# A fused attention and ReGLU kernel: batch 2 loaded last and transposed by the crossbar, a new order for the head, and an output lag that grows from 14 to 18

## The chip, the cores and the metric

The kernel runs on one core of one Trainium2 chip. The metric is the device time of one execution in microseconds (us). The kernel before the change took 221.94 us, the median of three runs that lay between 221.68 and 222.19.

The engines have short names in the profile. PE is TensorE, which does the matrix multiplications; PEld is its weight load, which runs beside the multiplications. DVE is VectorE, ACT is ScalarE, POOL is GpSimd, SP is SyncE. Transfers (DMA) are issued from the queues of SP, ACT and POOL.

## The reference

There are B = 8 batches and H = 8 heads, S = 512 rows of x and Ns = 32 rows of state for each, with head size D = 64.

```python
scale = 1.0 / np.sqrt(D)
a = softmax(scale * x @ state.T)            # over the 32 states
xread = a @ state                           # (B, H, 512, 64)
a2 = softmax(scale * state @ x.T)           # over the 512 rows
sread = a2 @ x                              # (B, H, 32, 64)
t = concat([xread, sread], axis=2)          # (B, H, 544, 64)
t = t.transpose(0, 2, 1, 3).reshape(B * 544, 512)
gate = np.maximum(t @ w_gate, 0.0)          # w_gate, w_val: 512 x 1536
val = t @ w_val
out = (gate * val) @ w_out                  # w_out: 1536 x 512
```

## The kernel before, in words

**The algebra.** The rows of xread are never formed. Since `xread = a @ state`, the product `xread @ w_gate` is `a @ (state @ w_gate)`. For each batch the kernel computes U, the 32 state rows of every head times w_gate and w_val, and then multiplies the softmax weights with U. The scores of both softmaxes are the same numbers, so one exponential serves both.

**The steps.** The head of the kernel is written as a list of words. A word is a step, its arguments, and after `@` the PSUM banks that it takes. The steps are: `dx` load x of a batch, `dw` load columns of w_gate (0) or w_val (1), `ds` load the rest of the state, `do` load rows of w_out; these loads are issued on the queue of POOL. `stc`, `stT` and `sto` convert and transpose the state and copy it into `stT`. `xT` transposes x of a batch on PE and `xo` copies it out of PSUM; `xd` (`x_trans_dma`) does the whole transposition instead by a DMA transpose on the queue of SP. `sc` computes scores, `ex` their exponentials, `nr` and `nx` sums, reciprocals and the product. `aT` with `ao` transposes the softmax weights on PE into `ans`, and `ad` does it by a DMA transpose on SP's queue. `c` with `co`, and `u` with `uo`, compute U for some columns and copy it out of PSUM (`c` takes gate and value columns together). `gv` is a slice, below, with `re` (relu) and `mu` (the product gate times value). `o` is an output piece and `of` the copy and the write of a finished output tile. `xp` copies x into a padded buffer `xa` on POOL, `sr` multiplies the exponentials with it on PE, and `sn` normalizes the result on VectorE. `spin` is a matmul on zeros whose result is used by nothing.

**The slices.** The 1536 hidden columns are cut into NF = 12 slices of 128. Slice number g = 12 b + jf is batch b, columns 128 jf and up: four matmuls of 128x512 (gate and value, two halves of the contraction), the relu on ScalarE, the product on VectorE into `h_sb`. Numbers 96 to 107 are the twelve slices of the sread rows of all batches.

**The pieces.** The 512 rows of a batch make four output tiles of 128 rows. Each tile is a sum over 12 slices in one PSUM bank, in three pieces of four matmuls: piece 12 b + 3 t + q is third q of tile t of batch b. The first piece of a tile (q = 0) asks for a bank, and after the last (q = 2) `fin_x` copies the tile out on ScalarE and writes it from SP.

**The loop.** The word list ends after 28 slices and 10 pieces. From slice `first` = 28 on a loop runs (lines 496 to 508): the slice; then one piece if `piece <= g - lag`, with `lag` 18; then the units planned for this slice; and, in slices in `paired`, a second piece behind the units. The units of batch s = 2 and up: score halves of the batch s + 1 (`att_half`); in slices jf = 7 and 10 a block of three `u` units of that batch (`u_block`), each with one copy on ScalarE and one on VectorE; the load, the DMA transpose and the pad copy of later batches; and `sr` of one batch: batch 2 in slice (2, 7), batch 3 in (2, 10), and each batch b from 4 on in (b - 1, 10). Slices jf = 7 and 10 of batches 2 to 6 are the paired ones. For slice (2, 7) the units stand in the order `u_block`, then `sr`, and then comes the second piece.

**The banks.** There are eight PSUM banks. In the loop, slices, U units and scores take banks 0 to 5 in turn, and output tiles banks 6 and 7 in turn. `sr` asks for a "spare" bank (lines 85 to 89):

```python
elif kind == "spare":
    n = 6 + turn["o"] % 2
else:
    n = turn["r"] % 6 if kind == "r" else 6 + turn["o"] % 2
    turn[kind] += 1
```

**What sets the order.** Each engine runs its instructions in the order in which the program gives them; nothing reorders them. Waits between engines are put in from the data: an instruction that writes a buffer or a bank waits for the earlier instructions that read it. Each queue of transfers issues in its own order too. POOL has eight semaphores for its loads, so a load waits until the eighth load before it has landed. The state transposes of batches 4 to 7 (`state_T_dma`) go through SP and their copies (`state_out_dma`) through POOL, both as units of slices of batch 2. After the loop come the output tiles of the sread rows (`fin_s`), the last pieces of batch 7, and the last tile in four column parts (`out_last`).

Of the kernel before, what the change touches and what calls it, by code (L numbers as in the profile page):

```python
# [16 lines left out]
def kernel(  # L17
# [203 lines left out]
    def x_pad(b):  # L221

        v = xa[:, b % NX].rearrange("p (c h) d -> p h c d", c=NC)[:, :, :, 0:D]
        nc.gpsimd.tensor_copy(out=v, in_=xb[b])  # L224
# [107 lines left out]
    def fin_x(b, tsub, eng="act"):  # L332
        o_sb = opool.tile([128, d_model], FP32, name="o_sb", tag="o_sb")
        copy[eng](out=o_sb, in_=held["o", b, tsub])  # L334
        n = 2 if 4 * B - 9 <= 4 * b + tsub < 4 * B - 4 else 1
# [74 lines left out]
    dx.1.0.2 dx.1.1.2 stc.0.0.act stc.0.1.act xc.0.0.dve dw.0.0.128 spin.7 stT.0@4 xc.0.1.act dw.1.0.128 on xT.0.0.4@2  # L410
    sto.0.0.dve sto.0.1.act xT.0.4.4@5 xo.0.0.4.dve dw.0.128.128 xo.0.4.4.dve dw.1.128.128 spin.1 sc.0.0@3 dw.0.256.256 ex.0.0 xT.0.8.4@0
    xT.0.12.4@1 xo.0.8.4.dve dw.1.256.256 xo.0.12.4.act nr.0.0 spin.2 sc.0.1@6 dw.0.512.256 xT.1.0.8@4 ex.0.1 nx.0.0
    xo.1.0.8.act nr.0.1 dw.1.512.256 spin.2 xT.1.8.8@2 xo.1.8.8.dve sc.1.0@5 dw.0.768.256 ex.1.0 nx.0.1 dw.1.768.256
    spin.2 c.0.0.128@30 sc.1.1@1 co.0.0.128.0.act nr.1.0 aT.0.1@6 co.0.0.128.1.act dw.0.1024.256 aT.0.0@4 ex.1.1
    ao.0.0.dve ao.0.1.act dw.1.1024.256 spin.1 c.0.128.128@25 c.1.0.128@30 nr.1.1 co.0.128.128.1.act gv.0.0@14
    co.0.128.128.0.act co.1.0.128.1.act nx.1.0 re.0.0 dw.0.1280.256 c.1.128.128@65 nx.1.1 gv.0.1@20 co.1.0.128.0.act
    co.1.128.128.0.act mu.0.0 co.1.128.128.1.act aT.1.1@7 re.0.1 dw.1.1280.256 aT.1.0@1 ao.1.1.act c.0.256.256@36
    ao.1.0.dve c.1.256.256@54 mu.0.1 co.0.256.256.0.act gv.1.1@21 dx.2.0.1 co.1.256.256.0.act co.0.256.256.1.dve
    re.1.1 gv.1.0@73 co.1.256.256.1.act mu.1.1 ds re.1.0 c.1.512.256@05 c.0.512.256@62 co.1.512.256.1.dve
    co.1.512.256.0.act gv.1.2@41 co.0.512.256.1.act mu.1.0 do.0.6 co.0.512.256.0.act gv.0.3@70 re.1.2 xp.1 gv.1.5@52  # L420
    re.0.3 mu.1.2 re.1.5 mu.0.3 gv.0.4@36 mu.1.5 re.0.4 xp.0 c.1.768.256@47 c.0.768.256@15 mu.0.4 co.1.768.256.0.act
    gv.0.2@03 co.0.768.256.0.act co.1.768.256.1.dve re.0.2 gv.0.5@26 do.6.12 co.0.768.256.1.act mu.0.2 gv.1.7@41 dx.3.0.1
    re.0.5 re.1.7 mu.0.5 gv.0.7@70 mu.1.7 re.0.7 gv.1.3@53 mu.0.7 re.1.3 gv.1.4@24 mu.1.3 re.1.4 gv.1.6@61 mu.1.4
    re.1.6 c.1.1280.256@70 c.0.1280.256@53 mu.1.6 co.1.1280.256.0.act c.1.1024.256@24 stc.1.0.pool xT.2.0.8@6
    co.0.1280.256.0.act co.1.1024.256.0.dve xT.2.8.8@1 co.0.1280.256.1.act co.1.1024.256.1.dve stc.1.1.pool
    c.0.1024.256@75 xo.2.8.8.act gv.0.10@23 co.1.1280.256.1.dve stc.3.1.pool co.0.1024.256.1.dve re.0.10 gv.1.9@40
    co.0.1024.256.0.act xo.2.0.8.dve stc.2.0.pool re.1.9 gv.0.6@12 mu.0.10 stc.3.0.pool re.0.6 mu.1.9 gv.0.11@57 mu.0.6
    stc.2.1.pool re.0.11 gv.0.8@64 mu.0.11 re.0.8 stT.1@3 gv.1.10@10 mu.0.8 sto.1.0.act sto.1.1.dve re.1.10 sc.2.0@2 o.0.0@7 ex.2.0
# [116 lines left out]
```

## Time and profile before

| what | value |
|---|---|
| median of three runs | 221.94 us (221.68 to 222.19) |
| the profiled execution, its own time | 222.66 us |
| the profiled execution, its span | 220.9 us |
| PE busy | 214.6 us, 97% of the span |
| DVE busy, ACT busy | 130.8 us, 123.5 us |
| a 128x512 matmul of `gv` or of an output piece | 380 ns each, the next starts 0.216 us after it |
| relu of a slice, product of a slice | 586 ns, 689 ns |
| landing of an x load of 512 KB, median | 7.1 us after its issue |
| landing of a weight load of 256 KB, median | 9.4 us (w_gate), 10.0 us (w_val) |
| landing of a DMA transpose of x | 4.4 to 8.0 us |
| landing of a DMA transpose of `ans` | 3.1 to 4.9 us |

A row of the profile in order of time begins with the start in us from the start of the span and the length in us; then follow the engine, the line of the kernel, the operation, the tile written and the tiles read, the shapes, and the number of instructions merged into the row. In brackets stand the idle time before the row and what ended it. Matmuls overlap, so a row of several matmuls ends later than the next row begins, and the pace of PE is read from start to start. The span is that of one execution; the device time of the same execution is 1.76 us longer.

### The profile page before, as it was taken

How to read it: one execution, taken by the hardware profiler on the slowest of the kernel's cores; microseconds unless marked ns; L12 is line 12 of the kernel's file. 1: busy time of each engine (PE TensorE's matmuls, PEld its weight loads, DVE VectorE, ACT ScalarE, POOL GpSimd, SP SyncE). 2: the span in 40 equal slices, each digit the busy share in tenths (PEclk: the TensorE clock that was granted, in tenths of full speed). 3: DMA queues.
4: the chain of work that ended last, by engine and by line, in shares of the span. 5: the costliest groups of instructions: out<-in, count | busy, mean ns of one | idle time of the engine just before them, and what ended most of it. 6: DMA issues, size and time to landing. Idle time of an engine off the chain costs nothing.

```text
span 220.9 us, 4858 instructions
## 1 busy us (share of the span) xinstructions
PE 214.6 (97%) x1955; PEld 105.2 (48%) x1955; DVE 130.8 (59%) x229; ACT 123.5 (56%) x236; POOL 40.6 (18%) x51
## 2 busy tenths in 40 slices
PE   7899999999999999999999999999999999999994
PEld 2553454444544444444444444445454445666543
DVE  5796898865787567664766487648665334222100
ACT  4699887465666565555566555646654543223221
POOL 7875830080035400040003000000000000000000
PEclk9999999999999999999999999999999999999999
DMA  7999999579057993655353105501411122222132
GB/s 165 165 195 197 198 241 204 52 213 167 8 127 112 185 142 98 142 96 103 85 130 83 50 19 142 121 16 43 112 37 53 47 47 50 50 57 85 50 95 96
DMA packets 42215, 23.65 MB, mean 107 GB/s; under 512 B 22640, under 2 KB 37872, under 8 KB 42192
## 3 DMA queue, kind: packets, MB, share of 16 engines
q0 software_dynamic: 16896, 9.05, 30.4%
q1 hardware_dynamic: 24400, 13.54, 24.3%
q10 hardware_dynamic: 896, 0.75, 1.4%
q8 instruction: 15, 0.25, 0.5%
q14 instruction: 8, 0.07, 0.1%
HBM read 18.35 MB, written 8.91 MB: 123 GB/s over the span
## 4 chain that ended last, share of the span: by engine, by line
PE 89%; DMA 7%; issue 1%; DVE 1%; POOL 1%; POOLq 0%
PE o_ps L326 39%; PE gv_ps L289 36%; PE gv_ps L306 5%; PE up L262 4%; DMA wv_sb<-in_moe_w_val_dram 4%; DMA xb<-in_x_dram 3%; PE sc_ps L170 1%; PE sr_ps L232 1%; PE o_ps L355 1%; PE upc L262 1%; PE xT_ps L156 0%; POOL xb L394 0%; DVE h_sb L317 0%; DVE stT L134 0%; POOL id masks.py:199 0%
## 5 line engine op out<-in xcount | busy, mean ns | idle before, releaser
L326 PE MATMUL o_ps<-wo_sb,h_sb 128*128 128x512 bf16 x372 | 94.6, 380 | 0.0
L289 PE MATMUL gv_ps<-ans,U 128*128 128x512 bf16 x384 | 94.1, 380 | 0.0
L317 DVE TENSOR_TENSOR h_sb<-gv_ps,g_sb 128x512 bf16<-128x512 f32 x96 | 65.3, 689 | 45.2 <-ACT g_sb L313 44.1
L313 ACT ACTIVATE g_sb<-gv_ps 128x512 bf16<-128x512 f32 (+1 forms) x108 | 63.0, 586 | 44.9 <-PE gv_ps L289 33.8
L289 PEld LDWEIGHTS <-U 128*128 128x128 bf16 x384 | 36.3, 98 | 42.2 <-issue 0.4
L326 PEld LDWEIGHTS <-h_sb 128*128 128x128 bf16 x372 | 35.3, 98 | 40.8 <-issue 2.1
L224 POOL COPY xa<-xb 128x2048 bf16<-128x2048 bf16 x8 | 15.1, 1898 | 69.2 <-PE sr_ps L232 52.2
L334 ACT COPY o_sb<-o_ps 128x512 f32<-128x512 f32 x31 | 18.3, 590 | 16.8 <-PE o_ps L326 14.8
L274 DVE CAST U<-up 128x512 bf16<-128x512 f32 x36 | 22.7, 685 | 5.7 <-PE up L262 5.6
L274 ACT CAST U<-up 128x512 bf16<-128x512 f32 x36 | 18.9, 594 | 12.1 <-PE up L262 12.0
L177 ACT ACTIVATE e_sn<-sc_ps 128x512 bf16<-128x512 f32 x16 | 9.6, 599 | 10.6 <-PE sc_ps L170 10.6
L317 DVE TENSOR_TENSOR hs_sb<-gv_ps,g_sb 128x256 bf16<-128x256 f32 x12 | 5.1, 425 | 15.1 <-PE gv_ps L306 9.2
L183 DVE TENSOR_REDUCE cs<-e_sn 128x16 f32<-128x512 bf16 x16 | 10.9, 681 | 4.4 <-ACT e_sn L177 4.4
L189 DVE TENSOR_TENSOR a_sn<-e_sn,rc 128x512 bf16<-128x512 bf16 x16 | 10.9, 686 | 0.4
L262 PEld LDWEIGHTS <-stT 64*32 64x32 bf16 x560 | 6.3, 90 | 9.6 <-issue 8.3
L284 ACT CAST U<-upc 128x512 bf16<-128x512 f32 (+1 forms) x21 | 10.0, 551 | 1.1 <-PE upc L262 1.1
L170 PEld LDWEIGHTS <-xT 128*128 128x128 bf16 x128 | 5.8, 98 | 4.4 <-issue 0.9
L262 PE MATMUL up<-wg_sb,stT 64*32 64x512 bf16 (+1 forms) x168 | 7.3, 349 | 0.0
L262 PE MATMUL up<-wv_sb,stT 64*32 64x512 bf16 (+1 forms) x168 | 7.3, 349 | 0.0
L170 PE MATMUL sc_ps<-stT,xT 128*128 128x64 bf16 x128 | 6.7, 193 | 0.5 <-DVE stT L134 0.3
L306 PE MATMUL gv_ps<-br,wg_sb 128*128 128x256 bf16 x48 | 7.2, 273 | 0.0
L306 PE MATMUL gv_ps<-br,wv_sb 128*128 128x256 bf16 x48 | 7.2, 273 | 0.0
(54 smaller groups left out, 112.9 us busy)
## 6 DMA issues: line engine op xcount, KB each, us to landing
out_dram<-o_sb SPq DMA_DIRECT2D x26, 256.0 KB, 2.4
xb<-in_x_dram POOLq DMA_DIRECT2D x6, 512.0 KB, 7.1
wo_sb<-in_moe_w_out_dram POOLq DMA_DIRECT2D x2, 768.0 KB, 13.5
out_dram<-o_sb SPq DMA_DIRECT2D x11, 128.0 KB, 2.4
wg_sb<-in_moe_w_gate_dram POOLq DMA_DIRECT2D x5, 256.0 KB, 9.4
wv_sb<-in_moe_w_val_dram POOLq DMA_DIRECT2D x5, 256.0 KB, 10.0
xb<-in_x_dram POOLq DMA_DIRECT2D x3, 256.0 KB, 5.9
st_f<-in_state_dram POOLq DMA_DIRECT2D x1, 384.0 KB, 11.5
```

What stands on the lines that cost most here:

```text
L170: nc.tensor.matmul(ps[:, h % 2, 2 * k:2 * k + 2, h // 2 % 2], xT[b][:, 2 * h + k], stT[:, b, h], start=True, stop=True)
L183: nc.vector.reduce_sum(out=cs, in_=e_v, axis=AX.X)
L189: {"dve": nc.vector, "pool": nc.gpsimd}[eng].tensor_tensor(out=by_pair(a_sn[b], jp).rearrange("p r (j n) -> p r j n", n=Ns), in0=e_v, in1= ...
L224: nc.gpsimd.tensor_copy(out=v, in_=xb[b])
L262: nc.tensor.matmul(dst[parity][32 * j:32 * j + 32], stT[r:r + 64, b, 2 * j + parity, 32 * parity:32 * parity + 32], wsb[r:r + 64, j, lo:lo ...
L274: copy[eng](out=U[b][:, w, kc, lo:lo + 512], in_=held["u", b, w, lo][kc])
L289: nc.tensor.matmul(ps[w], U[b][:, w, kc, f0:f0 + 128], ANS[b][:, kc].rearrange("p c t -> p (c t)"), start=(kc == 0), stop=(kc == NK - 1))
L306: nc.tensor.matmul(ps[w][:, 0:nt], wsb[:, j, f0:f0 + 128], br[:, j].rearrange("p b n -> p (b n)"), start=(j == 0), stop=(j == NJ - 1))
L313: nc.scalar.activation(out=g_sb[:, 0:n], in_=ps[0][:, 0:n], func=AF.Relu)
L317: nc.vector.tensor_tensor(out=dst, in0=ps[1][:, 0:n], in1=held["g", b, jf][:, 0:n], op=ALU.mult)
L326: nc.tensor.matmul(held["o", b, tsub], src[:, jf, tsub * 128:(tsub + 1) * 128], wo_sb[:, jf], start=(jf == 0), stop=(jf == NF - 1))
L334: copy[eng](out=o_sb, in_=held["o", b, tsub])
```

## The change

Five things change together.

1. The head is a new list of words in another order, with other banks. After x of batches 0 and 1 come all columns of w_gate and w_val, as before, then the rest of the state, w_out, x of batch 3, and last x of batch 2, which stood before the state. It is not transposed on PE (`xT.2` and `xo.2` are gone) but by the DMA transpose `xd.2` on SP. There are 19 `spin` matmuls for 15, and 14 output pieces for 10; the 28 slices are the same.
2. `lag` begins at 14 and grows by one at the slices jf = 1 of batches 4 to 7, until it is 18. The condition for a piece is the same.
3. The turn of banks 6 and 7 begins at 0 for 1, and the turn of banks 0 to 5 goes through them as 4, 1, 5, 2, 3, 0.
4. In the loop the state transposes and copies and the load of x of batch 4 are planned for other slices: the copies of state group 2 in slice (2, 5), ahead of the load of batch 4, and those of group 3 in (2, 11).
5. `x_pad` copies in two halves, and one more output tile is written in one transfer for two.

```diff
--- before.py
+++ after.py
@@ -76,7 +76,7 @@
     xf, xb, xT, e_sn, a_sn, ANS, U, hsb, sr_sb = {}, {}, {}, {}, {}, {}, {}, {}, {}
     copy = {"act": nc.scalar.copy, "dve": nc.vector.tensor_copy, "pool": nc.gpsimd.tensor_copy}
 
-    given, turn = [], {"r": 0, "o": 1}
+    given, turn = [], {"r": 0, "o": 0}
 
     def bank(name, kind="r"):
 
@@ -85,7 +85,7 @@
         elif kind == "spare":
             n = 6 + turn["o"] % 2
         else:
-            n = turn["r"] % 6 if kind == "r" else 6 + turn["o"] % 2
+            n = (4, 1, 5, 2, 3, 0)[turn["r"] % 6] if kind == "r" else 6 + turn["o"] % 2
             turn[kind] += 1
         return psum.tile([128, 512], FP32, name=name, tag=f"b{n}")
 
@@ -221,7 +221,8 @@
     def x_pad(b):
 
         v = xa[:, b % NX].rearrange("p (c h) d -> p h c d", c=NC)[:, :, :, 0:D]
-        nc.gpsimd.tensor_copy(out=v, in_=xb[b])
+        for hs in (slice(0, HK), slice(HK, H)):
+            nc.gpsimd.tensor_copy(out=v[:, hs], in_=xb[b][:, hs])
 
     def sr_mm(b, kind="r"):
 
@@ -332,7 +333,7 @@
     def fin_x(b, tsub, eng="act"):
         o_sb = opool.tile([128, d_model], FP32, name="o_sb", tag="o_sb")
         copy[eng](out=o_sb, in_=held["o", b, tsub])
-        n = 2 if 4 * B - 9 <= 4 * b + tsub < 4 * B - 4 else 1
+        n = 2 if 4 * B - 8 <= 4 * b + tsub < 4 * B - 4 else 1
         for i in range(n):
             rows = slice(128 // n * i, 128 // n * (i + 1))
             nc.sync.dma_start(out=out_rows(b, tsub)[rows], in_=o_sb[rows])
@@ -407,32 +408,33 @@
              "c": c_unit, "co": c_out, "u": u_unit, "uo": u_out, "gv": gv, "re": relu, "mu": mult, "o": out_part,
              "of": fin_x, "xd": x_trans_dma, "ad": att_aT_dma, "xp": x_pad, "sr": sr_mm, "sn": sr_norm}
     program = """
-    dx.1.0.2 dx.1.1.2 stc.0.0.act stc.0.1.act xc.0.0.dve dw.0.0.128 spin.7 stT.0@4 xc.0.1.act dw.1.0.128 on xT.0.0.4@2
-    sto.0.0.dve sto.0.1.act xT.0.4.4@5 xo.0.0.4.dve dw.0.128.128 xo.0.4.4.dve dw.1.128.128 spin.1 sc.0.0@3 dw.0.256.256 ex.0.0 xT.0.8.4@0
-    xT.0.12.4@1 xo.0.8.4.dve dw.1.256.256 xo.0.12.4.act nr.0.0 spin.2 sc.0.1@6 dw.0.512.256 xT.1.0.8@4 ex.0.1 nx.0.0
-    xo.1.0.8.act nr.0.1 dw.1.512.256 spin.2 xT.1.8.8@2 xo.1.8.8.dve sc.1.0@5 dw.0.768.256 ex.1.0 nx.0.1 dw.1.768.256
-    spin.2 c.0.0.128@30 sc.1.1@1 co.0.0.128.0.act nr.1.0 aT.0.1@6 co.0.0.128.1.act dw.0.1024.256 aT.0.0@4 ex.1.1
-    ao.0.0.dve ao.0.1.act dw.1.1024.256 spin.1 c.0.128.128@25 c.1.0.128@30 nr.1.1 co.0.128.128.1.act gv.0.0@14
-    co.0.128.128.0.act co.1.0.128.1.act nx.1.0 re.0.0 dw.0.1280.256 c.1.128.128@65 nx.1.1 gv.0.1@20 co.1.0.128.0.act
-    co.1.128.128.0.act mu.0.0 co.1.128.128.1.act aT.1.1@7 re.0.1 dw.1.1280.256 aT.1.0@1 ao.1.1.act c.0.256.256@36
-    ao.1.0.dve c.1.256.256@54 mu.0.1 co.0.256.256.0.act gv.1.1@21 dx.2.0.1 co.1.256.256.0.act co.0.256.256.1.dve
-    re.1.1 gv.1.0@73 co.1.256.256.1.act mu.1.1 ds re.1.0 c.1.512.256@05 c.0.512.256@62 co.1.512.256.1.dve
-    co.1.512.256.0.act gv.1.2@41 co.0.512.256.1.act mu.1.0 do.0.6 co.0.512.256.0.act gv.0.3@70 re.1.2 xp.1 gv.1.5@52
-    re.0.3 mu.1.2 re.1.5 mu.0.3 gv.0.4@36 mu.1.5 re.0.4 xp.0 c.1.768.256@47 c.0.768.256@15 mu.0.4 co.1.768.256.0.act
-    gv.0.2@03 co.0.768.256.0.act co.1.768.256.1.dve re.0.2 gv.0.5@26 do.6.12 co.0.768.256.1.act mu.0.2 gv.1.7@41 dx.3.0.1
-    re.0.5 re.1.7 mu.0.5 gv.0.7@70 mu.1.7 re.0.7 gv.1.3@53 mu.0.7 re.1.3 gv.1.4@24 mu.1.3 re.1.4 gv.1.6@61 mu.1.4
-    re.1.6 c.1.1280.256@70 c.0.1280.256@53 mu.1.6 co.1.1280.256.0.act c.1.1024.256@24 stc.1.0.pool xT.2.0.8@6
-    co.0.1280.256.0.act co.1.1024.256.0.dve xT.2.8.8@1 co.0.1280.256.1.act co.1.1024.256.1.dve stc.1.1.pool
-    c.0.1024.256@75 xo.2.8.8.act gv.0.10@23 co.1.1280.256.1.dve stc.3.1.pool co.0.1024.256.1.dve re.0.10 gv.1.9@40
-    co.0.1024.256.0.act xo.2.0.8.dve stc.2.0.pool re.1.9 gv.0.6@12 mu.0.10 stc.3.0.pool re.0.6 mu.1.9 gv.0.11@57 mu.0.6
-    stc.2.1.pool re.0.11 gv.0.8@64 mu.0.11 re.0.8 stT.1@3 gv.1.10@10 mu.0.8 sto.1.0.act sto.1.1.dve re.1.10 sc.2.0@2 o.0.0@7 ex.2.0
-    mu.1.10 nr.2.0 sc.2.1@5 gv.0.9@34 ex.2.1 re.0.9 nx.2.0 o.0.1 mu.0.9 gv.1.11@12 nr.2.1 xd.3 re.1.11 o.0.2 mu.1.11
-    o.0.3@6 nx.2.1 ad.2 of.0.0.act u.2.0.1024@05 u.2.1.512@34 uo.2.0.1024.0.dve uo.2.0.1024.1.act sr.0@1 sr.1@2
-    uo.2.1.512.1.act sn.0 u.2.0.0@50 sn.1 xp.2 xp.3 o.0.4 uo.2.0.0.0.act uo.2.0.0.1.dve uo.2.1.512.0.dve
-    o.0.5 o.0.6@7 of.0.1.act u.2.1.0@12 u.2.0.512@50 uo.2.1.0.0.act uo.2.1.0.1.dve u.2.1.1024@34 o.0.7
-    uo.2.1.1024.0.act uo.2.1.1024.1.dve uo.2.0.512.0.act gv.1.8@12 uo.2.0.512.1.dve re.1.8 o.0.8 mu.1.8
-    o.0.9@6 of.0.2.act gv.2.0@45 re.2.0 gv.2.2@01 mu.2.0 re.2.2 gv.2.1@23 mu.2.2 re.2.1 gv.2.3@45 mu.2.1
-    re.2.3 mu.2.3
+    stc.0.0.dve stc.0.1.act dx.1.0.2 dx.1.1.2 spin.7 stT.0@0 xc.0.0.dve xT.0.0.4@1 xc.0.1.dve sto.0.1.dve
+    xT.0.4.4@2 sto.0.0.act xo.0.0.4.act xo.0.4.4.act spin.3 sc.0.0@3 dw.0.0.128 dw.1.0.128 dw.0.128.128
+    dw.1.128.128 ex.0.0 dw.0.256.256 dw.1.256.256 dw.0.512.256 dw.1.512.256 dw.0.768.256 dw.1.768.256 dw.0.1024.256
+    dw.1.1024.256 dw.0.1280.256 on dw.1.1280.256 ds do.0.6 xp.1 xp.0 spin.1 xT.0.8.4@4 xT.0.12.4@5 nr.0.0
+    stc.2.1.pool stc.3.0.pool do.6.12 stc.1.1.pool dx.3.0.1 nx.0.0 stc.1.0.pool dx.2.0.1 stc.2.0.pool stc.3.1.pool
+    xo.0.8.4.act spin.2 xT.1.0.8@6 xo.1.0.8.dve xo.0.12.4.act sc.0.1@0 ex.0.1 spin.1 xT.1.8.8@1 sc.1.0@2
+    xo.1.8.8.act nr.0.1 ex.1.0 nx.0.1 spin.3 sc.1.1@3 ex.1.1 c.1.0.128@45 c.0.0.128@06 aT.0.1@1 aT.0.0@2 nr.1.0
+    co.0.0.128.1.act ao.0.1.dve nr.1.1 nx.1.0 co.0.0.128.0.act ao.0.0.act spin.1 c.0.128.128@36 spin.1
+    c.1.128.128@01 co.0.128.128.0.act nx.1.1 co.0.128.128.1.act co.1.128.128.1.act xd.2 co.1.0.128.1.act
+    co.1.0.128.0.dve gv.0.0@23 re.0.0 co.1.128.128.0.act gv.0.1@76 aT.1.0@1 aT.1.1@5 re.0.1 c.0.256.256@20
+    c.1.256.256@47 ao.1.0.dve ao.1.1.dve co.0.256.256.0.act co.1.256.256.1.act co.0.256.256.1.dve mu.0.0 mu.0.1
+    gv.1.0@15 gv.1.1@20 re.1.0 mu.1.0 re.1.1 c.1.512.256@73 c.0.512.256@16 gv.0.2@25 co.1.512.256.1.dve
+    co.0.512.256.1.dve co.1.512.256.0.act gv.0.3@73 co.1.256.256.0.act re.0.2 mu.0.2 re.0.3 co.0.512.256.0.act
+    gv.1.2@46 re.1.2 gv.1.4@27 mu.0.3 mu.1.1 gv.0.5@51 re.1.4 re.0.5 mu.1.2 c.1.768.256@34 c.0.768.256@02 mu.1.4
+    c.0.1024.256@67 mu.0.5 co.1.768.256.1.act gv.1.5@51 co.0.768.256.0.dve co.0.1024.256.0.dve co.0.768.256.1.act
+    gv.0.4@42 re.1.5 gv.1.3@05 co.0.1024.256.1.act re.0.4 c.1.1280.256@67 mu.1.5 co.1.768.256.0.dve mu.0.4 re.1.3
+    c.0.1280.256@14 mu.1.3 co.0.1280.256.0.dve c.1.1024.256@30 co.1.1280.256.0.act co.0.1280.256.1.act gv.0.6@26
+    re.0.6 gv.0.7@54 co.1.1024.256.1.act co.1.1024.256.0.act gv.0.10@12 re.0.10 re.0.7 co.1.1280.256.1.dve
+    gv.1.7@70 gv.1.11@31 mu.0.6 mu.0.7 gv.1.8@65 re.1.8 re.1.11 mu.0.10 re.1.7 mu.1.8 gv.1.6@42 gv.1.9@63 re.1.9
+    re.1.6 mu.1.7 mu.1.9 stT.1@5 sto.1.0.dve mu.1.6 mu.1.11 gv.0.9@76 sto.1.1.act gv.0.11@04 re.0.9 gv.0.8@35
+    re.0.11 u.2.1.512@72 u.2.0.0@01 mu.0.11 mu.0.9 re.0.8 uo.2.0.0.0.act uo.2.1.512.1.act sr.1@3 sr.0@4 sn.0
+    o.0.3@6 xp.3 xp.2 gv.1.10@04 o.0.4 sn.1 uo.2.1.512.0.dve mu.0.8 o.0.5 of.0.1.act uo.2.0.0.1.dve re.1.10 o.0.0@7
+    u.2.0.1024@23 u.2.1.0@51 u.2.0.512@60 uo.2.0.1024.1.dve uo.2.1.0.1.dve uo.2.0.512.0.dve o.0.1 o.0.2 sc.2.1@3
+    uo.2.1.0.0.dve ex.2.1 o.0.9@6 sc.2.0@1 o.0.10 u.2.1.1024@53 nr.2.1 ex.2.0 uo.2.0.1024.0.act of.0.0.act o.0.11
+    uo.2.0.512.1.act of.0.3.act o.1.0@7 o.0.6@6 o.1.1 o.0.7 o.0.8 nx.2.1 nr.2.0 nx.2.0 ad.2 gv.2.0@12 re.2.0
+    uo.2.1.1024.0.dve gv.2.2@05 xd.3 mu.2.0 mu.1.10 gv.2.3@12 uo.2.1.1024.1.act re.2.2 mu.2.2 re.2.3 gv.2.1@30
+    mu.2.3 re.2.1 of.0.2.act mu.2.1
     """
     for word in program.split():
         word, _, banks = word.partition("@")
@@ -468,12 +470,13 @@
         sr_mm(b, "spare")
         sr_norm(b)
 
-    first, lag = 2 * NF + 4, 18
-    at(2, 6, x_load, 4, 0, 1)
+    first, lag = 2 * NF + 4, 14
     for g in (2, 3):
         at(2, 2 + g, state_T_dma, g)
-        at(2, 8 + g, state_out_dma, g, 0, "pool")
-        at(2, 8 + g, state_out_dma, g, 1, "pool")
+    for half in range(2):
+        at(2, 5, state_out_dma, 2, half, "pool")
+        at(2, 11, state_out_dma, 3, half, "pool")
+    at(2, 5, x_load, 4, 0, 1)
     for b in range(3, B):
         s = b - 1
         for i, jf in enumerate((4, 5) if b == 3 else (3, 4)):
@@ -495,6 +498,8 @@
     piece = first - lag
     for g in range(first, NF * (B + 1)):
         b, jf = divmod(g, NF)
+        if lag < 18 and g >= 4 * NF and jf == 1:
+            lag += 1
         gv(b, jf) if b < B else gvs(jf)
         relu(b, jf)
         mult(b, jf)
```

## The prediction

> **What bounds the kernel now.** I read the page's engine shares first, then the order of time on TensorE, then its waits, then the order of time on all engines around the sum step `sr`. TensorE is the bound, at full granted clock:
>
> ```profile
> span 220.9 us, 4858 instructions
> PE 214.6 (97%) x1955; PEld 105.2 (48%) x1955; DVE 130.8 (59%) x229; ACT 123.5 (56%) x236; POOL 40.6 (18%) x51
> PEclk9999999999999999999999999999999999999999
> PE 89%; DMA 7%; issue 1%; DVE 1%; POOL 1%; POOLq 0%
> ```
>
> So what counts is idle time of TensorE and work added to or taken from it. The view of its waits from 45 to 206 us lists none: the loop is dense, and a wait put there is paid in full. Idle time exists only in the head. Its rows in order of time (start, length; a step's pace is start to start):
>
> ```profile
> 18.23 0.30 PE L262 MATMUL upc<-wg_sb,stT 64*32 64x256 bf16 x8
> 19.00 0.30 PE L262 MATMUL upc<-wv_sb,stT 64*32 64x256 bf16 x8 [0.46 <-DMA wv_sb<-in_moe_w_val_dram]
> 30.50 1.07 PE L156 MATMUL xT_ps<-id,xb 128*128 128x128 bf16 x16
> 31.50 0.30 PE L262 MATMUL upc<-wg_sb,stT 64*32 64x256 bf16 x8
> 36.39 1.03 PE L289 MATMUL gv_ps<-ans,U 128*128 128x512 bf16 x4
> 37.77 0.39 PE L170 MATMUL sc_ps<-stT,xT 128*128 128x64 bf16 x8 [0.35 <-DVE stT L134]
> 51.99 4.48 PE L289 MATMUL gv_ps<-ans,U 128*128 128x512 bf16 x20
> ```
>
> Up to 19.0 TensorE waits for weights: the unit for columns 512 to 767 stops until w_val lands. From 19.45 (its next `gv`) it runs on. A slice or an output piece is four matmuls of 0.216, 0.865 us. The loop's first slice, number 28, starts at 51.99 + 4 x 0.865 = 55.45, with 10 pieces done.
>
> The third stretch is the step `sr` of batch 2 in the loop:
>
> ```profile
> 63.35 0.45 PE L262 MATMUL up<-wg_sb,stT 64*32 64x512 bf16 x8
> 63.42 1.89 DVE L274 CAST U<-up 128x512 bf16<-128x512 f32 x3
> 63.73 0.43 PE L232 MATMUL sr_ps<-xa,e_sn 128*32 128x65 bf16 x32
> 64.10 1.04 PE L326 MATMUL o_ps<-wo_sb,h_sb 128*128 128x512 bf16 x4
> 65.22 0.16 DVE L239 RECIPROCAL rr<-sr_ps 128x2 f32<-128x2 f32 x1
> 65.42 0.29 DVE L241 TENSOR_TENSOR sn<-sr_ps,rr 128x128 bf16<-128x128 f32 x1
> ```
>
> TensorE goes from `sr` to an output piece at 64.10, while VectorE, busy with three casts of U, reads the bank of `sr` only until 65.71. That is harmless as long as the piece does not want that bank.
>
> **Part 1, the head.** *Removed from TensorE:* the 16 transposes of batch 2, 31.50 - 30.50 = 1.00 us, and the wait of 0.35 at 37.77 (the copy of stT for batches 2 and 3 is now followed by three slices before its first reader). Their two PSUM copies (1.04 on ScalarE, 0.68 on VectorE) go too; both engines had room. *Added:* four output pieces, 4 x 0.865 = 3.46, which the loop then does not do: no gain, no loss. Four more warm-up matmuls (19 for 15) lie before columns 512 to 767, where TensorE has until 19.0; adding the rows of ScalarE and VectorE along the new order (the last `ex` near 12.2, ans copied by 13.8, slices 0 and 1 to 15.6, the next transposes to 16.1, two more slices) I reach that unit at about 18.6: 0.4 of cover, and nothing gained, since the weights are issued in the same order. Without cover, a delay there would be paid one to one.
>
> From 19.45 to the loop before took 36.0 us; after, 36.0 - 1.00 - 0.35 + 3.46 = 38.1, so the loop starts at 57.55 where 55.45 + 3.46 = 58.91 would be break-even: a gain of 1.35, less three new waits.
>
> - *Weights.* By issue plus time to landing w_val 1024 lands at 24.4 and 1280 at 27.1. The new order asks for 1024 at 19.45 + 5 slices + two units of 0.22 = 24.2, and for 1280 at 27.3. Take 0.1; ends 0 and 0.5.
> - *x of batch 2, now last.* The same bytes follow the weights in another order: before, the last load landed at 40.9, 13.8 us after w_val 1280. GpSimd now holds the second w_out load behind two state casts, which wait for the state: 28.1 + 0.7 = 28.8, while the first w_out load still runs until 31.9, so the queue stays filled and x lands near 41.0. The crossbar step stands first in SP's queue; behind it wait the first output writes, whose buffers (8) do not run out. Its price before:
>
> ```profile
> 41.05 3.01 SPq L148 DMA_TRANSPOSE xT<-xb  x1
> xT<-xb SPq DMA_TRANSPOSE x1, 5.1
> ```
>
> So xT is there at 46.1 (45.4 at the 4.4 of three others, 49.0 at the 8.0 of one that ran beside a load). TensorE reaches the scores at 19.45 + 26.4 = 45.9 (20 slices, 6 pieces, 11 units, `sr` twice 0.65, stT 0.22, changeovers 4 x 0.12). Take 0.2; ends 0 and 3.1.
> - *ans of batch 2.* From the scores, counting from their start: exp at 0.43 to 1.03; sum, reciprocal and product of the two halves on VectorE to 4.4; SP also has to send the write of tile 3, whose copy ends at 4.2; the transpose goes at 4.7 and lands 3.2 later, 7.9 (8.9 behind the two writes, as the 4.9 of one such row suggests). TensorE has seven pieces, a unit and the other scores: 7.7. Take 0.4; ends 0 and 1.2.
>
> Behind it on SP, xT of batch 3 has 2.5 us before its scores in slice 28. The gain of the head: 1.35 - 0.7 = 0.65, ends 1.4 and, with all waits at their worst, -3.4.
>
> **Part 2, the lag.** Four slices (49, 61, 73, 85) give no piece while the lag grows; a lone `gv` keeps relu (0.59) and mult (0.69) within its 0.865: nothing. But the lag sets which piece stands where. A slice with a U block puts a second piece behind its units. With lag 18 the second piece in slice 12s+7 or 12s+10 is number 12s+7-18+1 or 12s+10-18+1: 2 modulo 3, the last third of a tile that holds its bank already. With lag 14 it is 0 modulo 3: a *new* tile, which takes the next of banks 6 and 7. `sr`, just ahead of it in the same slice, was given as "spare" exactly that bank, because asking for a spare does not advance the turn. So the first weight load of the piece waits until VectorE has read the sums (the built program has this wait, directly behind `sr`, four times; the old one nowhere). It hits `sr` of batch 2 (slice 31), 3 (34), 4 (46), and with lag 17 that of batch 7 (slice 82); lags 15 and 16 give second pieces of 2 and 1.
>
> What is queued behind: everything, since TensorE runs in order; ScalarE and VectorE then wait for it. Each price is from the same spot before, end of the VectorE read less start of the piece: 65.71 - 64.10 = 1.61; 72.18 - 70.52 = 1.66; 95.49 - 93.83 = 1.66; 165.41 - 163.76 = 1.65. To restart takes 0.12 (ans copied by 13.07, its `gv` at 13.19). Together 6.58 + 0.48 = 7.06. Ends: 4 x 0.6 = 2.4 if VectorE were free when `sr` ends (0.16 + 0.29 and two starts), 4 x 1.9 = 7.6 if its casts came 0.2 later. I take 7.06: the casts' order ahead of the read is unchanged.
>
> **Part 3, the rest.** The x_pad copies in halves run on GpSimd, idle at these times; tile 23 written in one transfer instead of two lies on SP, whose writes nobody waits for; the bank order in the loop stays a cycle of six. One chain moves far: GpSimd now issues the load of x of batch 4 behind the state copies of slice 29, and these wait for a state transpose on SP behind the first write of the loop, near 60.6 (issued at 52.4 before). Landing 2.5 to 4.1, copies 1.3, load 7.3, its crossbar 4.4 to 8.0: 76 to 81. Its scores stood at 79.17 and move by 2.8 and two stalls to 85.4: 4 us of cover, so nothing; without it a delay there is paid in full.
>
> **Sum.** The profiled run took 222.66, its span of 220.9 and 1.76 around it, 0.72 above the median of 221.94. 7.06 - 0.65 = +6.4: span 227.3, that run 229.1, the median 228.3.
>
> **Rivals.** (a) *Faster: the read of the sums is done in time.* Then only the head counts, 221.3, or 220.6 without its new waits. It decides from below 0.65 / 4 = 0.16 us a stall; the rows show 1.6, and the 1.89 of casts ahead of the read is on one engine in order. 0.05. (b) *The crossbar is late*, 8.0 us as beside a load: 2.9 more, 231.2. Against it: no load is left at 41. 0.07. (c) *The clock falls after each stall.* The first seven warm-up matmuls took 3.17, 0.453 each for 0.216 later; such a stretch after each stall adds 4 x 1.6 = 6.4: 234.7. For it: no gap over 0.5 us exists in the busy part, so the trace can't exclude it. 0.05. The Trainium skill bears on this, "TensorE: Matmul & The Clock Gate": its section "Why this matters for your kernels" puts the fall at idle gaps over about 3 us, by which these stalls are safe and the sum stays 228.3; its section "A second HAM failure mode: psum-queue depth-cycling" lets short idling between groups do it, by which 234.7. No run here shows either.
>
> **How the numbers follow.** The forecast has 0.82; 0.01 is left for a net of nothing. About 0.2% (0.45 us) is what a measurement of this kernel can tell from no change. Its own ends: small stalls 5.8 with 1.4 gained give 226.3; 7.6 with 1.0 lost gives 230.5. That range leaves out (a), (b), (c) and the like: 2 in 10. Slower 0.94, same 0.01, faster 0.05.
>
> **What would show it.** Right: four waits of TensorE of 1.7 us each for VectorE at the sums (L242), near 67, 75, 100 and 169 (their old times, moved by 2.8 for the later loop, by each stall before, and by 0.86 less for each of three pieces left out), ahead of output pieces; none of that length in the other two `sr` of the loop; slice 28 near 58.3; granted clock still full. Wrong: those waits missing or under 0.2, a wait over 1 us for xT or ans between 45 and 55, or matmuls at 0.45 behind a stall.

## The result, and the profile after the change

The changed kernel took 230.37 us, the median of six runs between 229.65 and 232.0; six runs of the kernel before had a median of 222.06 us. The ratio is 1.0379 (95% interval 1.0356 to 1.0402): 3.8% slower. The forecast was 228.3 us, the range 226.3 to 230.5. The profiled execution took 230.34 us, its span 228.6 us.

The page of the kernel after, busy times, the granted clock by fortieths of the span, and the shares of the chain that ended last:

```profile
span 228.6 us, 4801 instructions
...
PE 212.8 (93%) x1914; PEld 105.3 (46%) x1943; DVE 131.3 (57%) x231; ACT 121.2 (53%) x232; POOL 42.1 (18%) x59
...
PEclk9999999999999999999999999999999999999999
...
PE 83%; DVE 8%; DMA 4%; issue 2%; ACT 2%; DVEq 0%; ACTq 0%
```

TensorE does 1.8 us less work in a span 7.7 us longer, with a granted clock of 0.9 or more in every fortieth. So the loss is idle time, and the chain says on whom: VectorE, which had 1% of it, has 8%. The waits of TensorE (us in total, times, longest) name the places:

```profile
PE o_ps L327 <- DVE sn L242: 6.4, 4, 1.7
PE gv_ps L290 <- DMA ans<-a_sn: 1.3, 1, 1.3
...
PE sc_ps L170 <- DMA xT<-xb: 0.8, 1, 0.8
...
PE up L263 <- DVE h_sb L318: 0.2, 1, 0.2
```

The same waits in TensorE's order of time; brackets hold the idle time before a row:

```profile
19.35 0.82 PE L290 MATMUL gv_ps<-ans,U 128*128 128x512 bf16 x3
...
47.12 0.41 PE L170 MATMUL sc_ps<-stT,xT 128*128 128x64 bf16 x8 [0.80 <-DMA xT<-xb]
...
56.38 4.49 PE L290 MATMUL gv_ps<-ans,U 128*128 128x512 bf16 x20 [1.27 <-DMA ans<-a_sn]
...
70.56 1.04 PE L327 MATMUL o_ps<-wo_sb,h_sb 128*128 128x512 bf16 x3 [1.43 <-DVE sn L242]
...
78.70 1.04 PE L327 MATMUL o_ps<-wo_sb,h_sb 128*128 128x512 bf16 x3 [1.65 <-DVE sn L242]
...
103.73 1.04 PE L327 MATMUL o_ps<-wo_sb,h_sb 128*128 128x512 bf16 x3 [1.65 <-DVE sn L242]
...
172.78 1.04 PE L327 MATMUL o_ps<-wo_sb,h_sb 128*128 128x512 bf16 x3 [1.64 <-DVE sn L242]
```

The four last rows are the output pieces behind `sr` of batches 2, 3, 4 and 7. Before, such a piece began 0.37 after the start of `sr` (64.10 - 63.73). `sr` starts at 68.70, 76.62, 101.64 and 170.70 now; measured from 0.37 behind it the four begin 1.49, 1.71, 1.72 and 1.71 us late, 6.63 together. The row at 56.38 puts slice 28 at 56.38 + 4 x 0.865 = 59.84, where 58.91 was break-even: the head, which was to gain, lost 0.93. A further 0.57 was lost just ahead of the first `sr`, in the third U unit of slice 31. Here is that stretch on all engines:

```profile
65.30 1.28 POOL L130 COPY stT<-hs_sb 64x512 bf16<-64x512 bf16 x2 [20.53 <-DMA hs_sb<-st_b]
...
66.11 1.01 DVE L189 TENSOR_TENSOR a_sn<-e_sn,rc 128x512 bf16<-128x512 bf16 x1
...
67.04 1.27 DVE L318 TENSOR_TENSOR h_sb<-gv_ps,g_sb 128x512 bf16<-128x512 f32 x2
...
68.24 1.87 DVE L275 CAST U<-up 128x512 bf16<-128x512 f32 x3
...
68.36 0.41 PE L263 MATMUL up<-wg_sb,stT 64*32 64x512 bf16 x7 [0.19 <-DVE h_sb L318]
...
68.70 0.43 PE L233 MATMUL sr_ps<-xa,e_sn 128*32 128x65 bf16 x32
...
70.22 0.29 DVE L242 TENSOR_TENSOR sn<-sr_ps,rr 128x128 bf16<-128x128 f32 x1
```

The last two rows show the stall that was forecast: `sr` is done by 69.1, and VectorE, with the casts of U ahead in its order, reads the sums only at 70.22. The rows above show the one that was not. The product a_sn takes 1.01 us beside the second of two copies on GpSimd (it takes 0.69 elsewhere), so the next two products end late, and the third unit waits for the bank that one of them reads (from 67.31 to `sr` 1.39 us, where the other blocks take 0.82). The longer product gives 0.32 of these 0.57; the other 0.25 is a later VectorE, whose product starts 1.20 ahead of the first unit (67.31 - 66.11) and before started 1.45 ahead (62.91 - 61.46). Why it is later there is open.

0.93 + 0.57 + 6.63 = 8.13, and VectorE's last row starts 8.15 us later than before (225.51 for 217.36). The span is only 7.7 longer, as it ends 3.09 us behind that row and not 3.54. The medians differ by 8.31. The profiled run of the kernel before was itself 0.6 above its median, with a wait for weights near 19 us in the head that is shorter or missing in four other profiles with the same order up to there (the `gv` behind that wait stands at 19.45 there, and at 18.55, 18.60, 18.45 and 18.93 in the runs "before, with lag 17", "crossbar alone", the same with the first output piece ahead, and "one write" below). Positions within the head should be read with that spread of 1 us in mind.

### The profile page after: what moved, and what is told of

It is laid out like the page before. It is cut to its first block, busy times and chain, and to the rows that moved or that the text cites. A ratio compares the mean times of both kernels' runs of the same rounds, so it can differ in the third digit from the quotient of the medians.

```text
span 228.6 us, 4801 instructions
## 1 busy us (share of the span) xinstructions
PE 212.8 (93%) x1914; PEld 105.3 (46%) x1943; DVE 131.3 (57%) x231; ACT 121.2 (53%) x232; POOL 42.1 (18%) x59
## 4 chain that ended last, share of the span: by engine, by line
PE 83%; DVE 8%; DMA 4%; issue 2%; ACT 2%; DVEq 0%; ACTq 0%
PE gv_ps L290 35%; PE o_ps L327 33%; PE gv_ps L307 5%; DVE U L275 3%; PE up L263 3%; DMA ans<-a_sn 2%; DMA xT<-xb 2%; PE warm_ps L401 2%; DVE h_sb L318 2%; PE sc_ps L170 2%; PE upc L263 2%; PE o_ps L356 1%; DVE a_sn L189 1%; DVE cs L183 1%; ACT e_sn L177 1%
## 5 line engine op out<-in xcount | busy, mean ns | idle before, releaser
L327 PE MATMUL o_ps<-wo_sb,h_sb 128*128 128x512 bf16 x352 | 91.1, 379 | 8.1 <-DVE sn L242 6.4
L318 DVE TENSOR_TENSOR h_sb<-gv_ps,g_sb 128x512 bf16<-128x512 f32 x96 | 64.6, 688 | 51.3 <-ACT g_sb L314 50.7
L290 PE MATMUL gv_ps<-ans,U 128*128 128x512 bf16 x378 | 92.4, 379 | 1.6 <-DMA ans<-a_sn 1.3
L314 ACT ACTIVATE g_sb<-gv_ps 128x512 bf16<-128x512 f32 (+1 forms) x108 | 62.2, 581 | 56.6 <-PE gv_ps L290 45.3
L225 POOL COPY xa<-xb 128x1024 bf16<-128x1024 bf16 x16 | 16.1, 1041 | 58.1 <-PE sr_ps L233 36.0
L275 DVE CAST U<-up 128x512 bf16<-128x512 f32 x37 | 23.4, 684 | 5.5 <-PE up L263 5.5
L285 ACT CAST U<-upc 128x512 bf16<-128x512 f32 (+1 forms) x19 | 8.9, 531 | 1.2 <-PE upc L263 1.2
L401 PE MATMUL warm_ps<-hs_sb 128*128 128x512 bf16 x17 | 6.5, 508 | 1.2 <-DVE hs_sb L373 1.2
```

Source lines behind the costliest of these rows:

```text
L225: nc.gpsimd.tensor_copy(out=v[:, hs], in_=xb[b][:, hs])
L275: copy[eng](out=U[b][:, w, kc, lo:lo + 512], in_=held["u", b, w, lo][kc])
L290: nc.tensor.matmul(ps[w], U[b][:, w, kc, f0:f0 + 128], ANS[b][:, kc].rearrange("p c t -> p (c t)"), start=(kc == 0), stop=(kc == NK - 1))
L314: nc.scalar.activation(out=g_sb[:, 0:n], in_=ps[0][:, 0:n], func=AF.Relu)
L318: nc.vector.tensor_tensor(out=dst, in0=ps[1][:, 0:n], in1=held["g", b, jf][:, 0:n], op=ALU.mult)
L327: nc.tensor.matmul(held["o", b, tsub], src[:, jf, tsub * 128:(tsub + 1) * 128], wo_sb[:, jf], start=(jf == 0), stop=(jf == NF - 1))
```

## The experiments

Theory: the four stalls come from the place of a new output tile behind `sr`, whose bank was lent to `sr`, and make nearly the whole loss; the head lost by two late transfers. Rivals: the changed program slows the loop otherwise (banks, units), or the crossbar itself is to blame.

### The four stalls

**Another bank for `sr`**, in the changed kernel:

```diff
         elif kind == "spare":
-            n = 6 + turn["o"] % 2
+            n = 6 + (turn["o"] + (piece % 3 == 0)) % 2
```

> The changed kernel, but where the piece behind sr opens a new output tile, sr takes the other of banks 6 and 7, whose tile was finished ahead of it. Bank theory (TensorE waits four times for VectorE to read the sums out of the bank that the next tile wants): the four waits of 1.49 to 1.72 us, 6.63 in all, go, 230.4 - 6.6 = 223.7 us. Rival 1 (the loss sits in the new head, or in the lag as such, and the waits would only move elsewhere): 229 to 230.4 us. Rival 2 (a tile opened there is late because the tile before it has not been copied out by ScalarE): the wait stays at 1 us or more each and is named after ScalarE's copy, 228 us or more.

223.04 us, ratio to before 1.006 (1.0037 to 1.0084). No wait for L242 is left. One bank number takes back 7.3 of the 8.3 us. Of these, 6.63 are the stalls; in the profiles the other 0.65 lies ahead of the first `sr` (68.05 for 68.70), where x happened to land earlier and the scores did not wait for it.

**The kernel before, with lag 17** up to batch 6, and nothing else of the change:

```diff
-    first, lag = 2 * NF + 4, 18
+    first, lag = 2 * NF + 4, 17
...
-    piece = first - lag
+    piece = 10
...
+        if g == 7 * NF + 1:
+            lag += 1
```

> The kernel before, with nothing changed but the lag: 17 in place of 18, growing to 18 in slice 85. By the bank theory the second pieces behind sr of batches 3 to 7 now open a tile, so five waits of 1.7 us for VectorE's read of the sums appear in a kernel whose head is the old one: 222.1 + 5 x 1.72 = 230.7 us. Rival 1 (the loss is in the new head): 222.1 us, within 0.5.

230.55 us, ratio 1.0392 (1.0359 to 1.0425). Its waits of TensorE, and then two rows of its order of time:

```profile
PE o_ps L326 <- DVE sn L241: 8.2, 5, 1.6
```

```profile
72.23 1.04 PE L326 MATMUL o_ps<-wo_sb,h_sb 128*128 128x512 bf16 x4 [1.65 <-DVE sn L241]
...
172.32 1.04 PE L326 MATMUL o_ps<-wo_sb,h_sb 128*128 128x512 bf16 x4 [1.64 <-DVE sn L241]
```

Five stalls come out of the old head and old bank order by the number 17 alone, at the five `sr` of slices 12s+10. So the phase of the lag modulo 3 makes them, and no other part is needed.

**`sr` ahead of the U block**, in the changed kernel, with the same banks and lag:

```diff
         for part, jf in enumerate((7, 10)):
+            if jf == 10:
+                at(s, jf, sr, b)
+            elif s == 2:
+                at(s, jf, sr, 2)
             at(s, jf, u_block, b, part)
...
-        if b > 1:
-            at(s, jf, sr, b)
```

> The changed kernel with sr placed ahead of the three U units of its slice instead of behind them; banks as in the changed kernel, so the piece still wants the bank of the sums. Bank theory: the read of the sums now stands ahead of the three U casts on VectorE and ends about 0.75 us after sr, while TensorE has 0.78 us of U units to do: each wait shrinks to 0 to 0.2 us, 223.7 to 224.5 us. Rival (sharing the bank costs its time wherever the read stands): 229 to 230.4 us.

222.71 us, ratio 1.0035 (1.0022 to 1.0048). The conflict over the bank is still there; with VectorE's read ahead of its casts all that is left of the waits is small, 0.29 us in front of the piece's first weight load in slice 31 (at 68.11). The stall needed both, the shared bank and the casts ahead of the read.

**Another phase**: the changed kernel with lag 15, then 16, then 18.

```diff
-    first, lag = 2 * NF + 4, 14
+    first, lag = 2 * NF + 4, 15
...
-    piece = first - lag
+    piece = 14
...
-            lag += 1
+            lag += 2 if b == 6 else b == 5
```

> The changed kernel with 14 early pieces, but the lag goes 15, 16, 18 (no piece in slice 28, one slice without at batch 5, two at batch 6) instead of 14, 15, 16, 17, 18. By the bank theory the second pieces behind sr are then numbers 2, 2, 2, 2, 1 and 2 modulo 3 and none opens a tile: the four waits go, 223.7 us; two lone slices in a row may cost up to 0.5. Rival (pieces that come earlier against the slices cost time by themselves): 228 us or more.

222.78 us, ratio 1.0031 (1.0014 to 1.0048), without a wait for L242. Three independent ways to part the new tile from the unread bank give the same 222.7 to 223.0 us. What is left, 0.3 to 0.6% over the kernel before, is the head's and, where `sr` stands behind the U block and the copies still run beside the product (the run with another bank), the 0.57 of slice 31 (its first unit at 66.66, `sr` at 68.05, again 1.39).

The run with another phase also parts two things that GpSimd did beside that product. There the copies had ended, and only the load was being issued:

```profile
65.77 0.88 POOL L395 DMA_DIRECT2D xb<-in_x_dram  x1
...
65.97 0.69 DVE L189 TENSOR_TENSOR a_sn<-e_sn,rc 128x512 bf16<-128x512 bf16 x1
```

The product took 0.69, it started 1.41 ahead of the first unit (67.38), and `sr` followed that unit after 0.87. So it is the copy and not the load that lengthens the product.

### The head

The next four runs start from "`sr` ahead of the U block" (222.71 us). In its profile `ans` is waited for 1.28 us; in the changed kernel, SP's order of time was this:

```profile
42.68 2.12 SPq L148 DMA_TRANSPOSE xT<-xb  x1
44.87 6.91 SPq L339 DMA_DIRECT2D out_dram<-o_sb  x3
51.82 1.44 SPq L197 DMA_TRANSPOSE ans<-a_sn  x1
53.37 3.08 SPq L148 DMA_TRANSPOSE xT<-xb  x1
```

Output writes stand right ahead of the transpose of `ans`, which landed 4.5 us after its issue, against 3.2 in the kernel before, where they were issued behind it.

**The writes of tiles 0 and 3 behind that transpose**: `fin_x` is parted into the copy and the write.

```diff
-    ... of.0.0.act o.0.11 uo.2.0.512.1.act of.0.3.act ... nx.2.0 ad.2 gv.2.0@12 re.2.0
+    ... ofc.0.0.act o.0.11 uo.2.0.512.1.act ofc.0.3.act ... nx.2.0 ad.2 ofw.0.0 ofw.0.3 gv.2.0@12 re.2.0
```

> The kernel with sr first (e3_sr_first), and the writes of output tiles 0 and 3 leave SP's queue behind the DMA transpose of ans of batch 2 instead of ahead of it; their copies stay where they were. Theory: these two writes hold that transpose up, both its issue (by 0.3 us) and its landing (4.5 us in place of 3.2), so the wait of TensorE of 1.3 us for ans goes: ratio to the kernel before 1.0035 - 1.3/222 = 0.998. Rival (the transpose takes 4.5 us there anyway, or what waits is the product on VectorE): the wait stays above 0.8 us, ratio 1.002 to 1.004.

222.2 us, ratio 1.0013 (0.9997 to 1.0028). `ans` lands 3.9 us after its issue and is waited for 0.37 us, for 1.28. The transpose goes out 0.28 earlier after the scores (4.41 for 4.69) and takes 0.6 less. The ratio of 0.998 that was expected did not come; in this profile x landed late again, and the scores waited 0.35 us for it.

**The state copies and the load of x of batch 4 back** to their old slices. Only the copies of group 2 and this load had moved; the state transposes and the copies of group 3 stand where they stood before the change.

```diff
+    at(2, 6, x_load, 4, 0, 1)
     for half in range(2):
-        at(2, 5, state_out_dma, 2, half, "pool")
+        at(2, 10, state_out_dma, 2, half, "pool")
...
-    at(2, 5, x_load, 4, 0, 1)
```

> The kernel with sr first, and the state copies and the load of x of batch 4 back in the slices of the kernel before. Theory: on GpSimd the state copies of slice 29 run beside a product on VectorE (1.01 us in place of 0.69) and so delay the slice's product and a bank that U wants; with them back the product takes 0.69 again. With sr first this is worth 0 to 0.3 us: ratio 1.002 to 1.0035. Rival (the 1.01 us has another cause): the product still takes 1.0 us.

222.51 us, ratio 1.0022 (1.0004 to 1.0039). The product of slice 31 on VectorE is back at its length:

```profile
65.44 0.69 DVE L189 TENSOR_TENSOR a_sn<-e_sn,rc 128x512 bf16<-128x512 bf16 x1
```

**x of batch 2 loaded ahead of x of batch 3**, by exchanging two words:

```diff
-    ... stc.1.1.pool dx.3.0.1 nx.0.0 stc.1.0.pool dx.2.0.1 stc.2.0.pool ...
+    ... stc.1.1.pool dx.2.0.1 nx.0.0 stc.1.0.pool dx.3.0.1 stc.2.0.pool ...
```

> The kernel with sr first, and the loads of x of batches 2 and 3 in swapped order. The x of batch 2 lands 1.3 to 2.6 us earlier. Where x landed at 41.4 us TensorE did not wait for xT, so by the theory that only ans is late nothing changes: ratio 1.0025 to 1.0035. Rival (the late x of batch 2 is what delays the scores and through them ans): ratio 0.999 to 1.001.

222.77 us, ratio 1.0031 (1.0019 to 1.0043): nothing by itself. The transpose of x goes out at 39.06 for 41.36, and TensorE waits for `ans` as long as before (1.34 us). In this pair x was not what the scores waited for.

**All three together.**

> All three at once. The loop's first slice then starts near 57.6 us, with 58.9 as break-even: ratio 1.0035 less 1.3 to 1.6 us, 0.996 to 0.998, faster than the kernel before by 0.4 to 0.9 us. Rival (the new head can't win, as the ans of batch 2 is always the last): 1.000 or more.

221.58 us against 221.99 of the kernel before in the same set, ratio 0.9977 (0.9964 to 0.999): a version that beats both, by a quarter of a per cent. Its page, and its row of batch 2's first slices:

```profile
span 219.5 us, 4801 instructions
```

```profile
54.51 4.49 PE L290 MATMUL gv_ps<-ans,U 128*128 128x512 bf16 x20 [0.27 <-DMA ans<-a_sn]
```

Slice 28 stands at 54.51 + 3.46 = 57.97, 0.94 ahead of break-even; the prediction's head was to bring it to 58.3. Which two of the three edits would do was not tried.

### The crossbar alone

Is the late load of batch 2's x needed? In the **kernel before, batch 2 transposed by the crossbar**, with x loaded where it was:

```diff
-    ... xT.2.0.8@6 ... xT.2.8.8@1 ... xo.2.8.8.act ... xo.2.0.8.dve ...
+    ... xd.2 ...
```

> The kernel before with one part of the change alone: batch 2 is transposed by the crossbar, its x loaded where it was, right behind the weights, and order, lag and state copies as before. Theory of the head (what the change lost there came from the late load of x of batch 2 and from the output writes ahead of the second crossbar transpose, not from the crossbar): the 16 transposes of batch 2 leave TensorE, 1.0 us, and the first scores of batch 2 stand near 36 to 37 us, so with x there near 29.8 us and 4.4 us for the transpose there is no wait; 221.0 us, ratio near 0.9955. Rival (a crossbar transpose beside loads takes longer; the one of batch 3 took about 8 us beside a load): it lands near 37.8 us, the scores wait about 1 us, and the ratio is 0.999 to 1.001, with a wait for xT in the profile.

231.53 us, ratio 1.0425 (1.0396 to 1.0454). Neither theory had this. The transfers issued from 25 to 36 us (bytes each, us from issue to landing):

```profile
wo_sb<-in_moe_w_out_dram POOLq DMA_DIRECT2D x1, 768.0 KB, 15.2
xb<-in_x_dram POOLq DMA_DIRECT2D x1, 512.0 KB, 18.6
xT<-xb SPq DMA_TRANSPOSE x1, 14.7
```

The row of the scores in TensorE's order of time:

```profile
44.11 0.61 PE L170 MATMUL sc_ps<-stT,xT 128*128 128x64 bf16 x8 [7.72 <-DMA xT<-xb]
```

And its windows of 2 us (behind the busy times and counts of the five engines stand the granted clock, the DMA share and GB/s):

```profile
38.00:40.00 2.00, 0.00 (x0) 0.00 (x0) 0.00 (x0) 0.00 (x0) 0.00 (x0) 0.61 1.30 157
40.00:42.00 2.00, 0.00 (x0) 0.00 (x0) 0.00 (x0) 0.00 (x0) 0.00 (x0) 0.50 1.34 189
...
48.00:50.00 2.00, 2.00 (x9) 0.81 (x8) 1.30 (x3) 0.34 (x1) 0.00 (x0) 0.83 0.00 0
50.00:52.00 2.00, 2.00 (x10) 0.78 (x8) 1.52 (x3) 1.18 (x2) 0.00 (x0) 1.00 0.00 0
```

The transpose, issued while weight and x loads filled the DMA engines, landed with the last of them, 14.7 us later; in the changed kernel, with no load left, it took 4.4. TensorE waited 7.72 us, its clock fell to 0.50 in that wait and stayed there until 48.7: some 4.6 us of work at half pace, 2.3 more. With the 1.35 saved this is 8.7 of the 9.5 us; the rest I have not placed.

**The same, with the first output piece ahead of those scores** (`o.0.0@7 sc.2.0@2` for `sc.2.0@2 o.0.0@7`):

> The run crossbar alone, with the first output piece put ahead of the first scores of batch 2, which is 1.1 us more for the transposes of x and of the state to land. Theory of the head: 0.35 us less than crossbar alone where that run had a wait there (the kernel before waits 0.35 us for the state's transpose in front of these scores); 220.6 us, ratio near 0.994. Rival (late crossbar): the piece covers the 1 us that the late transpose costs, so this run is 0.4 to 0.5% below crossbar alone, and still near 0.995.

230.53 us, ratio 1.0383 (1.0353 to 1.0412). The wait is 6.50 us, shorter by the piece and the wait for stT, and the clock falls again. So, as far as these two runs go, the place of the load in the change is what makes its crossbar transpose affordable: my theory, that the late load was the fault and the crossbar free, was the wrong way round.

### Two small terms

**One output tile in one write**, alone, in the kernel before (`4 * B - 8` for `4 * B - 9`):

> The kernel before with one part of the change alone: tile 23 is written in one transfer instead of two. It asks where the 0.45 us come from by which every run with the changed program ended sooner after the last VectorE copy (span end 3.09 us behind it, 3.54 in the kernel before). If this part gives them: 3.1 us there, and a ratio of 0.998. If not (the prediction costed this part at nothing): 3.5 us and 1.000, and the cause is elsewhere in the program.

221.97 us, ratio 0.9996 (0.9981 to 1.0012), and its span ends 3.56 us behind VectorE's last row: nothing, as predicted. Where the 0.45 us at the end of the changed programs come from stays open.

**Four warm-up matmuls less** in "all three together": `spin.3` becomes `spin.1` ahead of `sc.0.0` and of `sc.1.1`.

> The run with all three mends of the head, less four warm-up matmuls (two ahead of the first scores, two ahead of the fourth), so 15 in all as in the kernel before. It asks why the new head reaches the 512 to 767 columns at 18.7 to 18.8 us where the old order did so at 18.0 in a profile without the wait for weights. If the added warm-up matmuls cause it: about 0.7 us sooner (2 x 0.43 at the slow clock at most, and 0.2 for the others), ratio near 0.995. Rival (they stand where TensorE would wait for x, the copies out of PSUM and the exponentials anyway): the same place, new waits in front of the scores, and a ratio of 0.997 to 0.998 as before; a clock that rises later would make it slower.

222.57 us, ratio 1.0026 (0.9999 to 1.0054), with an unusually wide spread (221.25 to 224.36). The unit of columns 512 to 767 starts at 18.88, no sooner, and TensorE's waits for the copies of xT grow:

```profile
PE sc_ps L170 <- ACT xT L159: 1.5, 3, 0.9
```

In this profile the rival holds: the added warm-up matmuls fill time in which TensorE would wait for the copies out of PSUM. The spread has another part as well: in four of the twelve runs the mean granted clock was 0.992, while it was 1.00 in all twelve of "all three together". How much of the 1 us is the clock's and how much the waits' was not parted.

## Why the prediction came out as it did

**Part 2, the lag: right, in place, number and cause.** Four waits of 1.43 to 1.65 us for L242, at the `sr` of batches 2, 3, 4 and 7, and none at the others, with the clock full. Their sum was put at 7.06 and measured 6.63. The term was too large by its restart, taken at 0.12 and measured at 0.05 (from VectorE's end at 70.51 to the piece at 70.56), and further by the first stall, which came out at 1.49 and not 1.73. Both parts of the cause were shown apart: the bank (another bank, another phase, lag 17 in the old kernel) and the casts ahead of the read (`sr` first).

**Part 1, the head: wrong in sign.** A gain of 0.65 was put down, and against the profiled run 0.93 was lost. From the `gv` behind the 512 unit (19.35) to slice 28, the changed kernel took 40.49 us; less the two waits shown, 0.80 and 1.27, that is 38.42, near the 38.1 worked out. The two failing terms are the waits:

- *x of batch 2*: taken at 0.2, measured 0.80. The load landed at 42.65, not near 41.0; the 4.4 of the transpose then held. In other profiles it landed at 41.4, without a wait, and at 43.5: it varies by 2 us, within the ends that were set.
- *ans*: taken at 0.4, measured 1.27. I used a landing of 3.2 us and kept the 4.9 "behind the two writes" as the far end; in this order the transpose does stand behind writes and took 4.5. That row should have been the price. The far end was also added up wrongly: an issue at 4.7 and 4.9 to landing give 9.6 and not 8.9, so it was a wait of 1.9 and not of 1.2. The issue itself came as worked out, 4.70 behind the scores (51.82 - 47.12). The run with the writes behind it brought 3.9 and 0.37. That writes ahead are the whole cause of the longer landing is not shown: the six profiles that have them ahead show 4.5 to 4.6, but the one of "crossbar alone" shows 4.6 with none ahead.

The other term, nothing up to 19.0, also missed against typical runs of the old order, which pass that point at 18.45 to 18.93 and not at 19.45: the profiled execution had an avoidable weight wait, and subtracting its 0.72 at the end of the sum credited the new head with it once more. That is why the median came out 2.0 above the forecast though the profiled sum was only 1.2 off.

One of the signs of being wrong that the prediction named, a wait over 1 us for xT or ans between 45 and 55, came true but for its place: `ans` was waited for 1.27 us from 55.1 on. And that 230.37 still lies inside the range, 0.13 us below its end, is in part luck: the end of 230.5 allowed for 1.0 us lost in the head, a figure that the working does not derive, and 0.93 was lost there.

**Part 3: "Nothing" was wrong by one edit of five.** The load of batch 4 had the cover that was worked out, and the single write costs nothing (run above). But the state copies, moved to slice 29, ran on GpSimd beside a product on VectorE, and the 0.32 by which it grew came through to TensorE as a part of the 0.57 lost there. I had asked only who waits for the copies, not whom they slow down while they run.

**The rivals.** (a), the sums read in time, fell: with the bank shared the waits stood. (b), a late crossbar, did not happen at its price in the changed kernel (landing 4.4), but the mechanism is real, and far dearer than the 8.0 row: 14.7 beside the queued loads. (c), the clock falling behind each stall, fell: the clock stayed at 1.00 through four gaps of up to 1.65 us, and around the five in "before, with lag 17". The pace agrees, and it is the better witness, since the granted clock reads 1.00 even in the first 5 us, where seven warm-up matmuls took 0.453 each: behind each of the four stalls the piece of four matmuls took 0.87 to 0.88 from start to start. This holds for the profiled run. The slowest of the six, 232.0 us, had a mean granted clock of 0.993, the others 1.00; half the clock for 3.2 us would give both that mean and the 1.6 us by which it is over the median (an estimate from these two numbers). It has no trace, so whether a stall set that off is open. The Trainium skill, "TensorE: Matmul & The Clock Gate", section "Why this matters for your kernels", warns of gaps over about 3 us, and by that the stalls were rightly held to be safe. The runs here put the edge lower: in "crossbar alone" the clock falls about 2.0 us after the last matmul ended (36.4 to 38.4), with the piece ahead of the scores about 2.7 us after (37.1 to 39.8).

## What to carry to other kernels

Where one piece of work borrows a buffer without taking its turn, work out which other piece takes that buffer next: here the order depends on a lag modulo 3. A lag that starts at 14 instead of 18 costs 6.6 us in four places, and one of 17 costs 8.2 us in five, while the work of every engine stays the same. Price a transfer by the row that has the same neighbours in its queue and on the DMA engines, not by the median: the same transpose took 4.4 us alone and 14.7 behind queued loads. And when work is moved off the critical engine, look at what runs beside its new place; a copy that nobody waits for can still lengthen an instruction that somebody waits for.

## What the runs showed of the hardware

- A VectorE product of two 128x512 bf16 tiles in SBUF took 0.69 us alone and 1.01 us with a GpSimd copy of a 64x512 tile beside it. The Trainium skill, "SBUF — State Buffer", section "Who interferes with whom", says that such a product contends with a GpSimd instruction that reads SBUF, and that the ports they share are an exclusive lock. The trace agrees but for a remainder: the product started at 66.11, the copy ended at 66.58 and the product at 67.12. Two more cases have the same end. Beside a pad copy of 128x1024 the same product took 1.33 (another bank, at 85.55) and 1.54 (`sr` first, at 85.25), and each time it ended 0.54 to 0.55 behind the copy, whenever it had started; so 0.55 of its 0.69 were left to do. Where the product started first (the run with the writes behind the transpose, at 85.32) it took 0.69, and the copy behind it 1.58 instead of 1.04.
- The DMA transpose of `ans` of batch 2 landed in 4.5 to 4.6 us with output writes right ahead of it on SP's queue (six profiles). With the writes issued behind it, it took 3.2 in the order of the kernel before, 3.8 to 4.3 in the three runs with that queue order changed (the writes behind it, all three together, fewer warm-ups), and 4.6 and 4.0 in the two crossbar runs. What decides within that second group was not found. One of x in the head took 4.4 to 5.4 with no load left or the end of one beside it, and 14.7 with 768 KB of weights and 512 KB of x still on their way; in that run the x load took 18.6 for 15.0. Whether the transpose waits for its share or for its turn was not tried.
- The granted clock of TensorE outlasted idle gaps of 1.43 to 1.65 us nine times, and was at 0.50 from 2.0 and 2.7 us into two longer ones; it came back 4.6 and 3.0 us after work restarted.
